# Rounding weights 512 columns at a time, and halving the first products of a fused attention and feed-forward kernel

## The chip, the cores and the metric

The kernel runs on one core of a Trainium2 chip. The metric is the device time of one execution in microseconds (us). The core has five engines that work side by side and wait for each other by semaphores: TensorE (PE in a profile, with its weight loads as PEld), VectorE (DVE), ScalarE (ACT), GpSimd (POOL), and SyncE (SP), which only issues DMAs here.

## What is computed

```python
# q, k, v: 8 batches x 8 heads x 576 rows x 64
scores = (q @ k.T) / 8
kth = the 32nd largest of each row of scores
attn = softmax(scores, with everything below kth masked out)
x = (attn @ v), rows of all batches below each other: 4608 x 512
g = x @ w_gate                      # 512 x 1536
out = ((g * sigmoid(g)) * (x @ w_val)) @ w_out      # w_out: 1536 x 512
```

q, k, v and the weights are random; the weights come as 64-bit floats, and the kernel rounds them to 32-bit ones on the chip.

## The kernel before

**Attention.** The work is cut into 160 units: (batch, query tile, pair of heads), with four tiles of 128 queries and a last one of 64 per batch, and four pairs of heads. A unit of the first four tiles has two heads (`nh` is 2); in a unit of the last tile, both heads lie in one set of 128 partitions, so it counts as one. The first batch's short units are 16 to 19. For a unit,

- `scores` (L276) makes the scores on TensorE (L306, or L292 for a short unit), and ScalarE copies them to `sc` (L311, L297);
- `select` (L314) finds the 32nd largest value on VectorE: four rounds of MAX8 (L327) with three of MATCH_REPLACE8 between them (L331), for each head, and then L337, which marks what lies below;
- `penalize` (L341) adds the marks to the scores on GpSimd (L349);
- `weigh` (L352) takes the exponentials on ScalarE (L358), and `normalize` (L366) divides by the sums (L370 on VectorE, L373 on ScalarE);
- `turn` (L375) transposes the result on TensorE (L385; ScalarE's copies are L386);
- `values` (L396) multiplies by v (L405, L414), and ScalarE copies the result into `xT[kb]` (L429). `done[kb]` counts the columns that are there.

`fetch` brings a batch's k and q: `load` issues the DMAs and `prep` transposes them on TensorE (L261, L253).

**Feed-forward.** The 4608 rows of x are 18 blocks of 256, which don't line up with the 576 rows of a batch. `feed(kb)` makes block kb: for each of six slices s of 256 hidden columns a gate product and a value product (`product`, L468, both [128 x 2 x 256] into a PSUM tile of `ps_f`, which has three), three ScalarE operations on the gate (L493 to L495), one on the value (L500), and two multiplications on GpSimd (L496, L501). Then comes the product with `wo`: plain for block 0 (L514), and in seven products of quarter size for the others (`quarter`, L554), with factors `T` that GpSimd makes from `wo` once. `feed` is a generator; each `yield` ends a piece and gives its size: 1 for four matmuls of 256 columns or two of 512, 0.75 for three of the quarters' matmuls.

**Rounding.** `rounded` (L105) takes one piece of a weight matrix, 128 rows x 256 columns, through five stages: the DMA (L109), two ScalarE operations (L114, L116), one on GpSimd (L119), one on VectorE and one on GpSimd (L123, L126), and a last one on VectorE (L129). `weights` makes 72 pieces, gate and value in turn for each 256 hidden columns and then `wo`, and sets them off as a pipeline: step n starts piece n and takes earlier ones through a later stage by `lags`. `ready[0]` counts the finished pieces. `rounding(n)` makes n steps; `need(n)` makes as many as it takes until n pieces are ready. `early[0]` moves the ScalarE stage of the newest pieces ahead. Loaded weights have six buffers `w`, and the sizes six.

**The order.** No scheduler moves anything: the four engines execute their instructions in the order in which the program names them. The loop at L705 makes one pass for each unit n; "step n" is that pass. In it stand, in this order: GpSimd's `penalize(n-1)`, TensorE's `turn(n-3)`, `values(n-4)` and `scores(n+1)`, ScalarE's `weigh(n-1)` and score copies, and then VectorE's `select(n)` in seven portions by `dve(k)`, between which pieces of the feed-forward work are placed by `pieces(k)`. `dve` lets 5/11 of a rounding step fall due for each selection operation, but none in the first four. `credit` limits the pieces: 4.45 are added in a step of two heads and 2.25 in a short one, and at most 8 are kept; from step 28 (`HEAD`) on `share(n)` takes the place of 4.45. ScalarE's and GpSimd's part of a product isn't placed at once but kept in `on_act` and `on_pool`, which `flush` empties; `piece` empties each of them first when it holds more than one entry:

```python
if len(on_act) > 1:
    flush(on_act)
if len(on_pool) > 1:
    flush(on_pool)
```

A block may begin when `done[kb]` says that all its columns are there. For block 0 these are units 0 to 7, which `values` finishes in step 11; for block 1 units 8 to 15 (step 19); block 2 takes in the last 64 rows of batch 0 and units up to 27 (step 31).

Of the kernel before, what the change touches and what calls it, by code (L numbers as in the profile page):

```python
# [8 lines left out]
AF = mybir.ActivationFunctionType  # L9
ALU = mybir.AluOpType  # L10
FP32 = mybir.dt.float32
I32 = mybir.dt.int32
# [3 lines left out]
P = 128  # L16
# [4 lines left out]
BLK = 256  # L21
WP = 256
# [5 lines left out]
def kernel(  # L28
# [37 lines left out]
    nc = tc.nc  # L66
    B, H, S, D = q.shape
    DM, DFF = w_gate.shape
# [17 lines left out]
    conv = ctx.enter_context(tc.tile_pool(name="conv", bufs=2))  # L86
# [17 lines left out]

    def rounded(src, dst):  # L105

        n = dst.shape[1]
        w = ffn.tile([P, n, 2], I32, tag="w", name="w", bufs=6)
        nc.sync.dma_start(w[:], src.bitcast(I32).rearrange("p (f t) -> p f t", t=2))  # L109
        yield  # L110
        low, high = w[:, :, 0], w[:, :, 1]

        size = conv.tile([P, n], FP32, tag="size", name="size", bufs=6)
# [9 lines left out]
        nc.vector.tensor_scalar(  # L123
            bits, bits, 3, 0x3FFFFFFF, ALU.logical_shift_left, ALU.bitwise_and
        )
        nc.gpsimd.tensor_tensor(bits, bits, low, ALU.add)  # L126
        yield

        nc.vector.scalar_tensor_tensor(  # L129
            out=dst.bitcast(I32), in0=high, scalar=-0x40000000, in1=bits,  # L130
            op0=ALU.bitwise_and, op1=ALU.bitwise_or,
        )

    def weights():

        pieces = []
        for f in range(0, DFF, WP):
            for src, dst in ((w_gate, wg), (w_val, wv)):
                for c in range(KC):
                    pieces.append((src[c * P : (c + 1) * P, f : f + WP], dst[:, c, f : f + WP]))  # L140
        for c in range(MC):
            for f in range(0, DM, WP):
                pieces.append((w_out[c * P : (c + 1) * P, f : f + WP], wo[:, c, f : f + WP]))
        pieces = [rounded(*p) for p in pieces]
        step = [0] * len(pieces)

        def upto(i, k):

            while 0 <= i < len(pieces) and step[i] < k:
                next(pieces[i], None)  # L150
                step[i] += 1

        lags = (5, 3, 2, 2, 0)
        for n in range(len(pieces) + lags[0]):
            for k, lag in enumerate(lags):
                upto(n - lag, len(lags) - k)
            ready[0] = max(n - lags[0] + 1, 0)
            early[0] = lambda: [upto(n - 1, 2), upto(n, 2)]
            yield
        early[0] = lambda: None  # L160


        add, sub = ALU.add, ALU.subtract
        lo, hi = slice(0, DM // 2), slice(DM // 2, DM)
        for m in range(0, MQ, 2):
            mm, nn = slice(m, m + 2), slice(MQ + m, MQ + m + 2)
            t3 = ffn.tile([P, 2, DM // 2], FP32, tag="w", name="t3", bufs=6)
            nc.gpsimd.tensor_tensor(t3[:], wo[:, nn, hi], wo[:, mm, hi], sub)
            T[7] += [t3[:, i, :] for i in range(2)]
            yield  # L170
        while not plain_done:
            yield
        for m in range(0, MQ, 2):
            mm, nn = slice(m, m + 2), slice(MQ + m, MQ + m + 2)
            t1 = wo[:, mm, hi]
            nc.gpsimd.tensor_tensor(t1, t1, wo[:, mm, lo], sub)
            T[5] += [wo[:, m + i, hi] for i in range(2)]
            yield
            t2 = ffn.tile([P, 2, DM // 2], FP32, tag="w", name="t2", bufs=6)
            nc.gpsimd.tensor_tensor(t2[:], wo[:, nn, hi], t1, sub)  # L180
            T[6] += [t2[:, i, :] for i in range(2)]
            yield
            for i in range(2):
                t4 = conv.tile([P, DM // 2], FP32, tag="size", name="t4", bufs=6)
                nc.gpsimd.tensor_tensor(t4[:], wo[:, MQ + m + i, lo], t2[:, i, :], sub)
                T[4].append(t4[:])
# [263 lines left out]
    def flush(queue):  # L450
        while queue:
            queue.pop(0)()

    def feed(kb):

        x = xT.pop(kb)
        hs = []  # L460

        def product(w, s, then):
            ps = ps_f.tile([P, 2, BLK], FP32, tag="f", name="f")
            need(8 * s + (4 if w is wg else 8))
            for i in range(2):
                m = 2 * s + i
                for kc in range(KC):
                    nc.tensor.matmul(  # L468
                        ps[:, i, :],
                        w[:, kc, m * P : (m + 1) * P],  # L470
                        x[:, kc, :],
                        start=(kc == 0),
                        stop=(kc == KC - 1),
                    )
                if i == 1:
                    on_act.append(lambda: then(ps))
                yield 1

        plain = kb == 0
        first, late = slice(0, P), slice(P, BLK)  # L480
# [2 lines left out]
            "p (m t) -> p m t", t=P  # L483
        )

        for s in range(MS):
            h = ffn.tile([P, 2, BLK], FP32, tag="h", name="h", bufs=MS + 1)
            hs.append(h)


            def gate(ps, h=h):
                half = ffn.tile([P, 2, BLK], FP32, tag="gv", name="half_g", bufs=3)
                nc.scalar.activation(h[:], ps[:], AF.Tanh, scale=0.5)  # L493
                nc.scalar.mul(half[:], ps[:], 0.5)
                nc.scalar.add(h[:], h[:], 1.0)  # L495
                on_pool.append(lambda: nc.gpsimd.tensor_mul(h[:], h[:], half[:]))  # L496

            def value(ps, h=h, s=s):
                val = ffn.tile([P, 2, BLK], FP32, tag="gv", name="val", bufs=3)
                nc.scalar.copy(val[:], ps[:])  # L500
                on_pool.append(lambda: nc.gpsimd.tensor_mul(h[:], h[:], val[:]))  # L501

            yield from product(wg, s, gate)
            yield from product(wv, s, value)
# [132 lines left out]
    current = []  # L637

    def piece():
# [4 lines that stand above are left out]
            flush(on_pool)  # L644
        while True:
            if not current:
                if not todo or done.get(todo[0], 0) < NHP * BLK:
                    return 0
                flush(on_act)
                flush(on_pool)  # L650
                current.append(feed(todo.pop(0)))
            cost = next(current[0], 0)
            if cost == 0:
                current.pop()
                continue
            return cost

    def fetch(n):

# [34 lines left out]
    load(1)  # L694
    run(fetch(0))
    run(scores(0))
    rounding(2)
    run(fetch(1))
    credit = [0.0]
    no = iter(())  # L700
    over = {}
    TURN, VALUES = 3, 4
    HEAD = 28
    due = [0.0]
    for n in range(NU + VALUES):  # L705
        nh = n_heads(units[n][1]) if n < NU else 1
        topk = select(n) if n < NU else no
# [106 lines left out]
```

## Time and profile before

| | us |
|---|---|
| device time, three runs | 1844.97, 1845.41, 1846.03 |
| the profiled run | 1845.35 |
| its span | 1843.6 |
| TensorE busy | 1708.1 (93%) |
| VectorE busy | 1623.5 (88%) |
| ScalarE busy | 1208.6 (66%) |
| GpSimd busy | 1026.2 (56%) |

Busy shares are means over stages with different limits. So the page also cuts the span into 40 slices of 46 us and gives the busy share of each engine in tenths (a digit 9 is 90% or more); PEclk in the same form is the clock that TensorE was granted. A table of windows gives, for each stretch, its length and then for PE, PEld, DVE, ACT and POOL the busy time with the number of instructions, then the granted clock, the busy share of the DMA engines and GB/s. The chain of work that ended last is followed back from the last instruction; its rows are start, length and what was done. A timeline has start, length, engine, line, operation, output and inputs, and in brackets how long the engine was idle before it, and what ended that. TensorE makes a matmul of 32-bit operands in two records, and a transpose in one.

### The profile page before, as it was taken

The page shows a single profiled execution, that of the slowest core. Times are in us where ns is not written, and L with a number is a line of the kernel's source. Part 1 is how long each engine was busy: PE and PEld are TensorE (multiplying, and loading weights), DVE is VectorE, ACT ScalarE, POOL GpSimd, SP SyncE. Part 2 cuts the span into 40 slices and gives each one's busy share as a digit, 9 for nine tenths or more (in the row PEclk, how much of TensorE's full clock was granted, in tenths as well). Part 3 has the DMA queues.
Part 4 walks back from the last instruction along what each step waited for, and adds up shares of the span by engine and source line. Part 5 has one row for each costly group of instructions (what it writes and reads, how often), then busy time and mean ns, then how long its engine had stood idle before and what let it go on. Part 6 is the DMA issues. An engine that isn't in the chain of part 4 may idle for free.

```text
span 1843.6 us, 30858 instructions
## 1 busy us (share of the span) xinstructions
PE 1708.1 (93%) x10756; PEld 1409.2 (76%) x10756; DVE 1623.5 (88%) x3477; ACT 1208.6 (66%) x3015; POOL 1026.2 (56%) x1007
## 2 busy tenths in 40 slices
PE   3447899999999989999999999999999999999998
PEld 2336658777788878887888878888788878888887
DVE  7999999999999979997999989998999989998400
ACT  5667757667666667676767675767676776675432
POOL 4666756645455644656464736564556554646444
PEclk7668999989999999999999999999999999999999
DMA  7332221000300021000300012000300011000000
GB/s 191 92 86 81 69 53 40 12 1 8 86 1 13 1 59 34 13 1 14 73 19 1 13 36 57 2 12 2 73 19 12 1 36 32 1 12 12 1 12 12
DMA packets 111260, 59.67 MB, mean 32 GB/s; under 512 B 89088, under 2 KB 97280, under 8 KB 111104
## 3 DMA queue, kind: packets, MB, share of 16 engines
q1 hardware_dynamic: 109904, 57.41, 11.8%
q8 instruction: 85, 1.39, 0.3%
q14 instruction: 71, 0.58, 0.1%
q10 hardware_dynamic: 1200, 0.30, 0.1%
HBM read 48.23 MB, written 9.44 MB: 31 GB/s over the span
## 4 chain that ended last, share of the span: by engine, by line
PE 83%; DVE 6%; ACT 3%; POOL 3%; issue 2%; DMA 0%; POOLq 0%; ACTq 0%
PE f L468 39%; PE x_ps L554 9%; PE av L414 8%; PE etps L385 7%; PE s L306 7%; PE y_ps L554 6%; DVE m L327 2%; DVE rest L331 2%; PE s L292 2%; PE av L405 1%; PE o_ps L514 1%; PE kqps L261 1%; POOL e L349 1%; ACT e L358 1%; DVE e L337 1%
## 5 line engine op out<-in xcount | busy, mean ns | idle before, releaser
L327 DVE MAX8 m<-rest 128x8 f32<-128x576 f32 x864 | 614.5, 745 | 2.2
L331 DVE MATCH_REPLACE8 rest<-m,rest 128x576 f32<-128x576 f32 x576 | 423.4, 741 | 0.0
L349 POOL TENSOR_TENSOR e<-e,sc 128x1152 f32<-128x1152 f32 (+1 forms) x160 | 382.7, 2392 | 67.2 <-DVE e L337 61.7
L468 PE MATMUL f<-xT,wg 128*128 128x256 f32 x1728 | 401.7, 382 | 0.0
L468 PE MATMUL f<-xT,wv 128*128 128x256 f32 x1728 | 398.9, 381 | 0.0
L468 PEld LDWEIGHTS f<-xT,wg 128*128 128x128 f32 x1728 | 322.8, 190 | 62.5 <-issue 20.5
L468 PEld LDWEIGHTS f<-xT,wv 128*128 128x128 f32 x1728 | 324.5, 190 | 58.5 <-issue 16.3
L496 POOL TENSOR_TENSOR h<-h,half_g 128x512 f32<-128x512 f32 x108 | 138.2, 1279 | 295.2 <-ACT h L495 289.6
L327 DVE MAX8 m<-sc 128x8 f32<-128x576 f32 x288 | 205.1, 748 | 99.1 <-ACT sc L297 58.3
L385 PE MATMUL etps<-ident,e 128*128 128x128 f32 (+1 forms) x1312 | 186.7, 287 | 104.3 <-POOL size L126 36.2
L358 ACT ACTIVATE e<-e,bias 128x576 f32<-128x576 f32 x288 | 222.1, 777 | 93.3 <-POOL e L349 93.2
L386 ACT COPY et<-etps 128x512 f32<-128x512 f32 (+1 forms) x448 | 184.3, 483 | 124.3 <-PE etps L385 122.9
L385 PEld LDWEIGHTS etps<-ident,e 128*128 128x128 f32 (+1 forms) x1312 | 159.6, 147 | 133.1 <-POOL size L126 39.0
L501 POOL TENSOR_TENSOR h<-h,val 128x512 f32<-128x512 f32 x108 | 140.2, 1298 | 193.2 <-ACT val L500 193.1
L373 ACT ACTIVATE e<-e,tot 128x576 f32<-128x576 f32 x288 | 211.9, 789 | 6.3 <-DVE tot L370 6.3
L331 DVE MATCH_REPLACE8 rest<-m,sc 128x576 f32<-128x576 f32 x288 | 211.6, 740 | 0.0
L306 PE MATMUL s<-kqT 64*128 64x288 f32 x1024 | 171.1, 447 | 4.4 <-ACT kqT L266 3.8
L414 PE MATMUL av<-et,v 128*64 128x128 f32 (+1 forms) x2560 | 173.8, 281 | 0.0
L337 DVE TENSOR_SCALAR e<-sc,m 128x576 f32<-128x576 f32 x288 | 165.4, 610 | 3.4
L311 ACT COPY sc<-s 128x288 f32<-128x288 f32 x512 | 163.9, 402 | 1.9 <-PE s L306 1.9
L414 PEld LDWEIGHTS av<-et,v 128*64 128x64 f32 x2560 | 136.8, 144 | 23.0 <-issue 7.1
L493 ACT ACTIVATE h<-f 128x512 f32<-128x512 f32 x108 | 65.4, 605 | 132.6 <-PE f L468 132.6
(71 smaller groups left out, 2042.1 us busy)
## 6 DMA issues: line engine op xcount, KB each, us to landing
kq_in<-in_k_dram SPq DMA_DIRECT2D x64, 128.0 KB, 2.8
v<-in_v_dram SPq DMA_DIRECT2D x32, 256.0 KB, 2.9
kq_in<-in_q_dram SPq DMA_DIRECT2D x62, 128.0 KB, 2.9
w<-in_moe_w_gate_dram SPq DMA_DIRECT2D x24, 256.0 KB, 2.7
w<-in_moe_w_val_dram SPq DMA_DIRECT2D x24, 256.0 KB, 2.7
w<-in_moe_w_out_dram SPq DMA_DIRECT2D x24, 256.0 KB, 2.5
out_dram<-o SPq DMA_DIRECT2D x40, 128.0 KB, 2.4
out_dram<-o SPq DMA_DIRECT2D x16, 256.0 KB, 2.4
```

The costliest lines, as they stand in the source:

```text
L306: nc.tensor.matmul(ps[:, 0:half], slab[d, q0 : q0 + P], slab[d, k0 : k0 + half])
L327: nc.vector.max(m[:, t, 8 * r : 8 * r + 8], cur[:, hs])
L331: nc.vector.match_replace(rest[:, hs], m[:, t, 8 * r : 8 * r + 8], cur[:, hs], LOWEST)
L337: nc.vector.tensor_scalar(e[:, hs], sc[:, hs], m[:, t, TOP_K - 1 : TOP_K], FAR, ALU.is_lt, ALU.mult)
L349: nc.gpsimd.tensor_tensor(e[:, every], e[:, every], sc[:, every], ALU.add)
L358: nc.scalar.activation(e[:, hs], e[:, hs], AF.Exp, bias=bias[:, t : t + 1], scale=scale, accum_out=tot[:, t : t + 1],)
L373: nc.scalar.mul(e[:, hs], e[:, hs], tot[:, t : t + 1])
L385: nc.tensor.transpose(ps[0:kl, c * P : (c + 1) * P], e[:, k0 : k0 + kl], ident[:])
L386: nc.scalar.copy(et[0:kl, c0 : c0 + cn, :], ps[0:kl, 0 : cn * P].rearrange("p (c j) -> p c j", c=cn),)
L414: nc.tensor.matmul(av[hh * R : (hh + 1) * R, 0:ql], v_last[:, hh, :] if c == J else vt[:, hh, c, :], moving, start=last and c == 0, stop=c ...
L468: nc.tensor.matmul(ps[:, i, :], w[:, kc, m * P : (m + 1) * P], x[:, kc, :], start=(kc == 0), stop=(kc == KC - 1),)
L554: nc.tensor.matmul(ps, lhsT, T[i][m], start=m == 0, stop=m == MQ - 1)
```

## The change

`rounded` takes pieces of twice the size: two row groups of 256 columns for gate and value weights, and a whole row group of 512 for `wo`. There are 36 of them, in three buffers of double size, and a step of the pipeline acts on a piece every second time, so that as many columns fall due as before. In the prelude k and q of the first pair of heads are split over the DMA queues by head, `rounding(2)` after the first scores is left out, and `due` starts at 2.0.

`parts` cuts the columns of blocks 0 and 1 into two halves of 128. `feed` makes all gate and value products of the first half and then those of the second, and a half may begin when its own columns are there: those of units 0 to 3 for block 0 (step 7), and of units 8 to 11 for block 1 (step 15). A half's piece has size 0.5, and `pieces` counts sizes, not pieces, so that two of 0.5 or two of 0.75 now go where one of 1 went.

`need`, which made rounding steps at once, becomes `until`, which yields 0 while weights are missing: then no piece is placed, and the next place for one tries again.

```diff
-        w = ffn.tile([P, n, 2], I32, tag="w", name="w", bufs=6)
+        w = ffn.tile([P, 2, WP, 2], I32, tag="w", name="w", bufs=3)
...
-                for c in range(KC):
-                    pieces.append((src[c * P : (c + 1) * P, f : f + WP], dst[:, c, f : f + WP]))
+                for c in range(0, KC, 2):
+                    rows = src[c * P : (c + 2) * P, f : f + WP]
+                    pieces.append((
+                        rows.rearrange("(c p) f -> p c f", p=P), dst[:, c : c + 2, f : f + WP]
+                    ))
...
-        for n in range(len(pieces) + lags[0]):
+        for n in range(2 * len(pieces) - 1 + lags[0]):
             for k, lag in enumerate(lags):
-                upto(n - lag, len(lags) - k)
-            ready[0] = max(n - lags[0] + 1, 0)
-            early[0] = lambda: [upto(n - 1, 2), upto(n, 2)]
+                if (n - lag) % 2 == 0:
+                    upto((n - lag) // 2, len(lags) - k)
+            ready[0] = max((n - lags[0]) // 2 + 1, 0)
+            early[0] = lambda: upto(n // 2, 2)
             yield
...
-    def need(n):
+    def until(n):
 
         while ready[0] < n:
-            next(weight)
+            yield 0
...
-            queue = nc.scalar if n == 1 and i == 0 else nc.sync
             for hh in range(2):
+                queue = nc.scalar if hh == 1 and i == 0 else nc.sync
                 queue.dma_start(
...
-            queue.dma_start(
+            nc.sync.dma_start(
                 kq_last[n * R : (n + 1) * R], src[b, h, JP:S].rearrange("h p d -> p h d")
...
+    def parts(kb):
+
+        return [slice(0, P), slice(P, BLK)] if kb < 2 else [slice(0, BLK)]
...
-        def product(w, s, then):
+        def product(w, s, c, then):
+            n = c.stop - c.start
+            yield from until(4 * s + (2 if w is wg else 4))
             ps = ps_f.tile([P, 2, BLK], FP32, tag="f", name="f")
-            need(8 * s + (4 if w is wg else 8))
...
-                yield 1
+                yield n / BLK
...
+        for c in parts(kb):
+            while done[kb] < NHP * c.stop:
+                yield 0
...
-                    need(8 * MS + 2 * m + 2)
+                    yield from until(4 * MS + m + 1)
...
-                if not todo or done.get(todo[0], 0) < NHP * BLK:
+                if not todo or done.get(todo[0], 0) < NHP * parts(todo[0])[0].stop:
                     return 0
...
     def pieces(n):
-        for _ in range(n):
-            if credit[0] >= 1:
-                credit[0] -= piece()
+        while n > 0 and credit[0] >= 1:
+            size = piece()
+            if not size:
+                break
+            n -= size
+            credit[0] -= size
...
-    rounding(2)
     run(fetch(1))
...
-    due = [0.0]
+    due = [2.0]
```

GpSimd's factors `T` get their room in the same three buffers (`room`), and its last subtraction, made for each of two row groups before, is made once for both.

More of the change, by code (lines that the diff above doesn't have):

```diff
@@ L105, in rounded @@
     def rounded(src, dst):
-        n = dst.shape[1]
-        w = ffn.tile([P, n, 2], I32, tag="w", name="w", bufs=6)
-        nc.sync.dma_start(w[:], src.bitcast(I32).rearrange("p (f t) -> p f t", t=2))
+        w = ffn.tile([P, 2, WP, 2], I32, tag="w", name="w", bufs=3)
+        nc.sync.dma_start(
+            w[:].rearrange("p c f t -> p c (f t)"), src.bitcast(I32)
+        )
         yield
-        low, high = w[:, :, 0], w[:, :, 1]
-        size = conv.tile([P, n], FP32, tag="size", name="size", bufs=6)
+        low, high = w[:, :, :, 0], w[:, :, :, 1]
+        size = conv.tile([P, 2, WP], FP32, tag="size", name="size", bufs=3)
         nc.scalar.activation(size[:], high.bitcast(FP32), AF.Abs)
@@ L138, in weights @@
             for src, dst in ((w_gate, wg), (w_val, wv)):
-                for c in range(KC):
-                    pieces.append((src[c * P : (c + 1) * P, f : f + WP], dst[:, c, f : f + WP]))
+                for c in range(0, KC, 2):
[3 more added lines that the diff above has]
+                    ))
         for c in range(MC):
-            for f in range(0, DM, WP):
-                pieces.append((w_out[c * P : (c + 1) * P, f : f + WP], wo[:, c, f : f + WP]))
+            pieces.append((
+                w_out[c * P : (c + 1) * P].rearrange("p (c f) -> p c f", c=2),
+                wo[:, c].rearrange("p (c f) -> p c f", c=2),
+            ))
         pieces = [rounded(*p) for p in pieces]
@@ L164, in weights @@
         lo, hi = slice(0, DM // 2), slice(DM // 2, DM)
+        room = []
+        for _ in range(3):
+            t = ffn.tile([P, 4, DM // 2], FP32, tag="w", name="t", bufs=3)
+            room += [t[:, 0:2], t[:, 2:4]]
         for m in range(0, MQ, 2):
             mm, nn = slice(m, m + 2), slice(MQ + m, MQ + m + 2)
-            t3 = ffn.tile([P, 2, DM // 2], FP32, tag="w", name="t3", bufs=6)
-            nc.gpsimd.tensor_tensor(t3[:], wo[:, nn, hi], wo[:, mm, hi], sub)
+            t3 = room.pop()
+            nc.gpsimd.tensor_tensor(t3, wo[:, nn, hi], wo[:, mm, hi], sub)
             T[7] += [t3[:, i, :] for i in range(2)]
@@ L178, in weights @@
             yield
-            t2 = ffn.tile([P, 2, DM // 2], FP32, tag="w", name="t2", bufs=6)
-            nc.gpsimd.tensor_tensor(t2[:], wo[:, nn, hi], t1, sub)
+            t2 = room.pop()
+            nc.gpsimd.tensor_tensor(t2, wo[:, nn, hi], t1, sub)
             T[6] += [t2[:, i, :] for i in range(2)]
             yield
[L183 to L186, printed above, removed]
+            t4 = conv.tile([P, 2, DM // 2], FP32, tag="size", name="t4", bufs=3)
+            nc.gpsimd.tensor_tensor(t4[:], wo[:, nn, lo], t2, sub)
+            T[4] += [t4[:, i, :] for i in range(2)]
             yield
@@ L222, in load @@
                 )
-            queue.dma_start(
+            nc.sync.dma_start(
                 kq_last[n * R : (n + 1) * R], src[b, h, JP:S].rearrange("h p d -> p h d")
@@ L452, in flush @@
             queue.pop(0)()
+    def parts(kb):
+        return [slice(0, P), slice(P, BLK)] if kb < 2 else [slice(0, BLK)]
     def feed(kb):
-        x = xT.pop(kb)
+        x = xT[kb]
         hs = []
-        def product(w, s, then):
+        def product(w, s, c, then):
+            n = c.stop - c.start
+            yield from until(4 * s + (2 if w is wg else 4))
             ps = ps_f.tile([P, 2, BLK], FP32, tag="f", name="f")
-            need(8 * s + (4 if w is wg else 8))
             for i in range(2):
@@ L468, in product @@
                     nc.tensor.matmul(
-                        ps[:, i, :],
+                        ps[:, i, 0:n],
                         w[:, kc, m * P : (m + 1) * P],
-                        x[:, kc, :],
+                        x[:, kc, c],
                         start=(kc == 0),
@@ L475, in product @@
                 if i == 1:
-                    on_act.append(lambda: then(ps))
-                yield 1
+                    on_act.append(lambda: then(ps[:, :, 0:n], c))
+                yield n / BLK
         plain = kb == 0
@@ L484, in feed, with gate, value @@
         )
[L486 to L504, printed above, removed]
+        for c in parts(kb):
+            while done[kb] < NHP * c.stop:
+                yield 0
+            for s in range(MS):
+                if c.start == 0:
+                    hs.append(ffn.tile([P, 2, BLK], FP32, tag="h", name="h", bufs=MS + 1))
+                h = hs[s]
+                def gate(ps, c, h=h):
+                    half = ffn.tile([P, 2, BLK], FP32, tag="gv", name="half_g", bufs=3)
+                    hc, gc = h[:, :, c], half[:, :, c]
+                    nc.scalar.activation(hc, ps, AF.Tanh, scale=0.5)
+                    nc.scalar.mul(gc, ps, 0.5)
+                    nc.scalar.add(hc, hc, 1.0)
+                    on_pool.append(lambda: nc.gpsimd.tensor_mul(hc, hc, gc))
+                def value(ps, c, h=h):
+                    val = ffn.tile([P, 2, BLK], FP32, tag="gv", name="val", bufs=3)
+                    hc, vc = h[:, :, c], val[:, :, c]
+                    nc.scalar.copy(vc, ps)
+                    on_pool.append(lambda: nc.gpsimd.tensor_mul(hc, hc, vc))
+                yield from product(wg, s, c, gate)
+                yield from product(wv, s, c, value)
+        del xT[kb]
         o = ffn.tile([P, 2, DM], FP32, tag="o", name="o", bufs=1)
@@ L651, in piece @@
                 current.append(feed(todo.pop(0)))
[L652 to L656, printed above, removed]
+            size = next(current[0], None)
+            if size is not None:
+                return size
+            current.pop()
     def fetch(n):
```

## The prediction

> **What bounds the kernel now.** I read part 2 of the page first, then windows of 20 us over the head, then groups, timeline and chain there. "Step n" is pass n of the loop at L705; it ends with VectorE's two L337 of unit n.
>
> ```profile
> PE   3447899999999989999999999999999999999998
> DVE  7999999999999979997999989998999989998400
> PEclk7668999989999999999999999999999999999999
> ```
>
> After its first tenth TensorE is full; before that it is not, while VectorE is.
>
> ```profile
> 100.00:120.00 20.00, 12.28 (x70) 9.85 (x70) 20.00 (x48) 14.42 (x39) 12.09 (x19) 0.60 0.36 104
> 120.00:140.00 20.00, 6.36 (x36) 5.13 (x37) 20.00 (x51) 12.63 (x34) 12.93 (x16) 0.65 0.29 79
> 140.00:160.00 20.00, 11.61 (x77) 9.66 (x78) 20.00 (x48) 14.49 (x40) 12.48 (x19) 0.75 0.33 108
> 160.00:180.00 20.00, 20.00 (x113) 17.22 (x112) 19.00 (x40) 13.29 (x33) 14.99 (x16) 1.00 0.17 54
> ```
>
> The third figure of busy time is VectorE: 20.00 of 20 up to 160 us. The feed-forward work starts at 158.8 us and fills TensorE. Reading VectorE's timeline step by step: step 31 starts at 380.9 us; steps 31 to 35 take 10.56 us each with no wait, a one-head step 6.25. With the 0.53 us that a rounded piece takes (below), the head's floor is 12.6 (VectorE's first start) + 27x10.56 + 4x6.25 + 72x0.53 = 361 us. So 20 us are lost up to 380.9: 4.0 in steps 0 to 10, 10.0 in 11 to 16, 5.2 in 17 to 30, and rounding.
>
> ```profile
> 354.23 0.98 PE etps L385 x9
> 355.21 0.22 PE av L405 x2
> 355.44 1.05 PE av L414 x16
> ...
> 365.27 1.17 PE s L306 x8
> 366.44 3.01 issue
> ...
> 383.47 1.71 PE f L468 x7
> ```
>
> In this chain no feed-forward row stands between 354 and 383 us: block 1 is done and block 2's columns need values of unit 27, made in step 31. So whatever block 1 gains is given back in a longer pause. The built order of the changed program bears this out: in steps 27 to 30 it has no product at all, from step 31 on TensorE has the same sequence as before but for four steps with an inner exchange. The change is worth what it does to the start of step 31, one for one.
>
> [...]
>
> ```profile
> 176.62 2.62 POOL L349 TENSOR_TENSOR e<-e,sc 128x1152 f32<-128x1152 f32 x1
> 177.35 2.17 DVE L129 SCALAR_TENSOR_TENSOR wo<-w,size 128x256 int32<-128x256 int32 x1
> 179.20 1.45 POOL L501 TENSOR_TENSOR h<-h,val 128x512 f32<-128x512 f32 x1
> 179.45 1.36 DVE L123 TENSOR_SCALAR size<-size 128x256 int32<-128x256 int32 x1
> ```
>
> The 0.40 us L129 takes 2.17 and ends with L349. [...] in the chain above TensorE's rows follow the program's order. [...] Trace: L129 starts 0.33 us before the next instruction, L123 0.20[...]. [...]
>
> **The change part by part.**
> (1) *512 columns a piece.* VectorE had 72 pairs at 0.33+0.20 us; it gets 36 at 0.60+0.33 (the same with twice the elements). 38.2-33.5 = 4.7 us saved, nearly all where VectorE is full. ScalarE and GpSimd save too (L114, L116 0.33 each to an estimated 0.55; L126 0.75 to 1.28 as L501's 512 columns take, L119 0.44 to 0.60), hidden behind VectorE. But GpSimd's add (L126), 1.28 us long then, starts as soon as L123 has ended, so where L337 comes right behind (units 3, 7 and 10), it waits some 1.2 us and not 0.7. Steps 0 to 6, which lose 2.7 now, lose an estimated 3.0.
> (2) *Prelude.* k and q split over SP's and ScalarE's queues: k's halves issue together (0.7 us each), 0.7 us earlier; kq_last's q half goes on SP behind the others, 0.6 us later. VectorE's first MAX8 no longer stands behind L123 (12.64 us), but its second wait, the first size operation, comes after fetch(1)'s copies on ScalarE: estimated 14.7 against 14.2 us with the same work done. Cost 0.5 (-0.7 to +1.5).
> (3) *DMAs.* Half as many, twice as large (512 KB), same bytes, three buffers for six. From a freed buffer to the size operation that needs its successor: issue and landing an estimated 4.6 (0.5, and 2.7 as the page's median plus 256 KB at its 191 GB/s), ScalarE 0.55, GpSimd 0.6, so 6 us against four rounding steps of 8 us. Nothing expected; up to 5 us lost. Queued behind it on SP are later loads and stores, 2.4 to 2.9 us to landing and due a step later.
> (4) *Halves.* Block 0 starts at step 7. A 256-column product record takes 0.216 us (8 in 1.73), a 128-column one 0.109 by the transposes: TensorE pays nothing. ScalarE's operation of 256 columns takes 0.33 us (L114's spacing) and of 512 0.49 (L493's), so a block's worth of 48 short for 24 long ones costs 4 us over ten steps; GpSimd's 0.75 twice for 1.28 costs 2.6. Both idle over 3 us a step. Upper bound, were loads to cost the 190 ns that their rows last: +31 us a block; the transposes exclude it nearly.
> (5) *A new order on GpSimd.* In step 8 (and 12, the same pattern for the second half) two half products fit into `pieces(2)`, so ScalarE's val and gate, and GpSimd's two multiplications, stand ahead of the size minimum of the next piece. In steps 7 and 11 eight such multiplications delay the 2.6 us add L349: as now in step 12, it starts 2.6 us into the step. From there in step 8: add ends 5.1, two exponentials 7.0, score copies 8.2, val and gate 9.5, multiplication 10.3, minimum 10.9 us. VectorE reaches the size operation that needs it after 8 selections and an L129: 6.2. It waits 4.7 us, twice: 9.4 (2.6 each if the add is on time, so 5 to 10). Other collisions and L337 in steps 7 to 16: 6.7 (the present 1.6 in 7 to 10 and 10.0 after it, with multiplications half as long).
> (6) *Not forced, due 2.0.* Forcing never happens in the steps that matter now: L129 runs 4 or 5 times in each. But w_out's twelve pieces now end at step 15: piece 10 after eight selections, piece 11 after thirteen (10.7 us into it). TensorE's order puts twelve o_ps matmuls into step 15, eleven of them not before that.
>
> ```profile
> 233.70 5.35 PE o_ps L514 x12
> 239.05 0.79 issue
> 239.84 1.38 PE etps L385 x9
> 241.22 0.22 PE av L405 x2
> 241.44 1.02 PE av L414 x16
> 242.47 1.12 PE s L292 x8
> ```
>
> Two records a matmul: 0.89 us. 11x0.89 = 9.8, so TensorE ends 20.5 us after step 15's start, 8.4 after step 16's. Then transposes 1.0, av 1.25, scores 1.1 and their copies 0.8: VectorE has its scores at 12.6, and wanted them at 6.25. It waits 6.3 us. TensorE then carries 6.1, 4.3, 4.5 and 4.5 us of products and transposes beside 3 of the unit's own in the short steps 16 to 19: further waits of 3.1, 1.3 and 1.4. Sum 12.1 (bounds 5, now, and 14). The two-head steps after it just keep pace (11 against 10.56 with the slack), and 27 to 30 have slack: 0.6.
> Sum up to step 31: floor 361-4.7+0.5 = 356.8; lost 3.0+9.4+6.7+12.1+0.6 = 31.8; 388.6 against 380.9: +7.7 us. The span of 1843.6 becomes 1851.3; its run was 1845.35, the others 1844.97 to 1846.03, so 1853.0 on their scale.
>
> **The rivals.**
> *Faster:* GpSimd's multiplications come in time and the o_ps burst is absorbed. VectorE keeps the 4.7, and TensorE, eleven pieces ahead by step 11, loses 1 us and not 5 in 17 to 30: 4.7-0.5+4 = 8 us, 1837. For it: VectorE is at 20.00 of 20, so each instruction saved there counts in full. Against: (5) and (6) follow from the order. It decides if VectorE's lost time up to step 31 stays below 20.0+4.7-0.5 = 24.2 us.
> *No change:* only one of (5) and (6) bites. Without (5), 7.7-9.4 = -1.7; without (6), 7.7-6.9 = +0.8: 1844 to 1846.
> *Slower yet:* both, and the larger DMAs arrive late in steps 1 to 6 (5 us), or half matmuls cost more than half: 1858 to 1863. TensorE's clock of 0.60 at 100 us speaks for it.
> *It doesn't do what it says* (no earlier start) is excluded: the 128-column rows stand ahead of step 8's transposes.
>
> **How the numbers follow.** Faster 0.20, no change 0.17, slower 0.63 (the forecast 0.48, slower yet 0.15). 0.2% (3.7 us) is about what a measurement can tell from no change. The range runs from 1840, inside the faster case, to 1862; about 2 in 10 lie outside.
>
> **What would show it.** Right: in the profile after, step 31 starts near 388 us with the rest as before; VectorE idles about 5 us before a size operation in steps 8 and 12 (releaser GpSimd's minimum), about 6 before a MAX8 in step 17 (releaser ScalarE's score copy); MAX8 stays at 0.745 us; 36 size operations at 0.33 to 0.45. Wrong: no such waits, or step 31 before 380; a difference made after step 31; 128-column product records spaced well over 0.11 us.

## The result, and the profile after

| | before | after |
|---|---|---|
| device time, median of five runs each, us | 1845.62 (1844.97 to 1846.03) | 1862.31 (1861.94 to 1864.73) |
| ratio, 95% interval | | 1.0092 (1.0078 to 1.0106) |
| span of the profiled run, us | 1843.6 | 1860.1 |
| start of step 31, us | 380.9 | 401.1 |

The changed kernel is slower by 16.7 us; 7.7 were forecast, and the range ended at 1862.0. Its direction was right and its size was not. Read off VectorE's timeline step by step (a step ends with its last marking, L349), the time went here (length of each stretch in us; the floor is VectorE's own work at 10.56 us a two-head step and 6.25 a one-head step):

| | before | after | difference |
|---|---|---|---|
| up to the end of step 6 | 105.9 | 103.0 | -2.9 |
| steps 7 to 16 | 134.8 | 139.1 | +4.3 |
| steps 17 to 20 (floor 29.3) | 31.1 | 46.2 | +15.1 |
| steps 21 to 30 (floor 105.6) | 109.1 | 112.8 | +3.7 |
| step 31 to the end | 1462.7 | 1459.0 | -3.7 |

In the table of windows of the changed kernel the third busy time is VectorE's again; before, it was 20.00 of 20 up to 160 us.

```profile
120.00:140.00 20.00, 11.64 (x79) 10.09 (x75) 14.69 (x32) 11.48 (x29) 14.05 (x14) 0.74 0.18 53
240.00:260.00 20.00, 20.00 (x138) 13.92 (x137) 8.32 (x15) 9.55 (x25) 5.69 (x6) 1.00 0.05 17
```

Two stretches now have VectorE idle: around 130 us with TensorE idle too, and around 250 us with TensorE at 20.00 of 20. The list of what VectorE waited for between 100 and 300 us (sum, times, longest) names two things:

```profile
DVE m L339 <- ACT sc L309: 13.7, 3, 8.8
DVE size L124 <- POOL size L120: 12.1, 5, 5.3
```

The second row is steps 8, 9 and 12, with 0.5 us in step 15. GpSimd's timeline of step 8, which begins at 118.4 us:

```profile
121.51 2.65 POOL L361 TENSOR_TENSOR e<-e,sc 128x1152 f32<-128x1152 f32 x1
124.11 1.20 POOL L518 TENSOR_TENSOR h<-h,half_g 128x256 f32<-128x256 f32 x1
127.77 0.73 POOL L524 TENSOR_TENSOR h<-h,val 128x256 f32<-128x256 f32 x1 [2.46 <-ACT val L523]
128.56 0.72 POOL L518 TENSOR_TENSOR h<-h,half_g 128x256 f32<-128x256 f32 x1
129.37 0.61 POOL L120 TENSOR_SCALAR size<-size 128x512 f32<-128x512 f32 x1
```

and VectorE's row that waits for the last of them, with the wait in brackets:

```profile
130.02 0.43 DVE L124 TENSOR_SCALAR size<-size 128x512 int32<-128x512 int32 x1 [5.31 <-POOL size L120]
```

The multiplications of step 7's products hold the add L361 until 121.51, 3.1 us into the step; the exponentials wait for the add, ScalarE's val (L523) stands behind the exponentials, and the minimum L120 behind that. The first row of the waits is steps 17 to 19. The chain after w_out's last pieces, where `233.70 5.35 PE o_ps L514 x12` was the longest run of o_ps before:

```profile
234.43 11.40 PE o_ps L538 x22
...
248.07 1.12 PE s L304 x8
```

Step 16 ended at 242.1, and VectorE got step 17's scores at 250.92. Of the chain ahead of block 2 this is left:

```profile
390.69 1.23 POOL e L361
...
403.00 8.83 PE f L485 x40
```

Block 2 begins right after step 31's start, as before, and from 358 to 403 us no product stands in the chain: blocks 0 and 1 are done early and nothing comes of it.

### The profile page after: what moved, and what is told of

It is laid out like the page before. It is cut to its first block, busy times and chain, and to the rows that moved or that the text cites. A ratio compares the mean times of both kernels' runs of the same rounds, so it can differ in the third digit from the quotient of the medians.

```text
span 1860.1 us, 31376 instructions
## 1 busy us (share of the span) xinstructions
PE 1719.8 (92%) x11140; PEld 1426.9 (77%) x11140; DVE 1616.4 (87%) x3405; ACT 1211.1 (65%) x2991; POOL 1020.6 (55%) x956
## 4 chain that ended last, share of the span: by engine, by line
PE 78%; POOL 3%; ACT 3%; DVE 2%; issue 1%; POOLq 0%; ACTq 0%; DVEq 0%
PE f L485 38%; PE x_ps L578 9%; PE av L426 7%; PE etps L397 7%; PE s L318 6%; PE y_ps L578 6%; PE s L304 2%; PE av L417 1%; DVE m L339 1%; DVE rest L343 1%; POOL e L361 1%; PE kqps L273 1%; PE o_ps L538 1%; ACT e L370 1%; POOL p L564 1%
## 5 line engine op out<-in xcount | busy, mean ns | idle before, releaser
L339 DVE MAX8 m<-rest 128x8 f32<-128x576 f32 x864 | 622.3, 765 | 2.2
L343 DVE MATCH_REPLACE8 rest<-m,rest 128x576 f32<-128x576 f32 x576 | 429.1, 761 | 0.0
L361 POOL TENSOR_TENSOR e<-e,sc 128x1152 f32<-128x1152 f32 (+1 forms) x160 | 382.9, 2393 | 82.6 <-DVE e L349 73.5
L485 PE MATMUL f<-xT,wv 128*128 128x256 f32 (+1 forms) x1920 | 408.1, 364 | 15.0 <-DVE wv L130 14.0
L485 PE MATMUL f<-xT,wg 128*128 128x256 f32 (+1 forms) x1920 | 406.9, 362 | 4.1 <-DVE wg L130 4.1
L485 PEld LDWEIGHTS f<-xT,wv 128*128 128x128 f32 x1920 | 337.0, 193 | 71.9 <-issue 18.3
L485 PEld LDWEIGHTS f<-xT,wg 128*128 128x128 f32 x1920 | 333.5, 191 | 62.2 <-issue 20.2
L518 POOL TENSOR_TENSOR h<-h,half_g 128x512 f32<-128x512 f32 (+1 forms) x120 | 141.7, 1181 | 308.0 <-ACT h L517 302.2
L524 POOL TENSOR_TENSOR h<-h,val 128x512 f32<-128x512 f32 (+1 forms) x120 | 143.5, 1196 | 199.5 <-ACT val L523 198.5
L385 ACT ACTIVATE e<-e,tot 128x576 f32<-128x576 f32 x288 | 212.3, 790 | 8.5 <-DVE tot L382 8.5
L349 DVE TENSOR_SCALAR e<-sc,m 128x576 f32<-128x576 f32 x288 | 170.7, 639 | 3.4
L515 ACT ACTIVATE h<-f 128x512 f32<-128x512 f32 (+1 forms) x120 | 67.9, 566 | 135.0 <-PE f L485 134.8
```

Source lines behind the costliest of these rows:

```text
L339: nc.vector.max(m[:, t, 8 * r : 8 * r + 8], cur[:, hs])
L343: nc.vector.match_replace(rest[:, hs], m[:, t, 8 * r : 8 * r + 8], cur[:, hs], LOWEST)
L349: nc.vector.tensor_scalar(e[:, hs], sc[:, hs], m[:, t, TOP_K - 1 : TOP_K], FAR, ALU.is_lt, ALU.mult)
L361: nc.gpsimd.tensor_tensor(e[:, every], e[:, every], sc[:, every], ALU.add)
L385: nc.scalar.mul(e[:, hs], e[:, hs], tot[:, t : t + 1])
L485: nc.tensor.matmul(ps[:, i, 0:n], w[:, kc, m * P : (m + 1) * P], x[:, kc, c], start=(kc == 0), stop=(kc == KC - 1),)
```

## The experiments

Theory A, the forecast's: the loss is one of order. Multiplications on GpSimd stand ahead of what VectorE needs (steps 8 and 12), o_ps comes as a burst (step 15), and GpSimd is late in steps 21 to 26; the larger pieces are a gain. Rivals: B, the larger pieces are slow themselves; C, half products cost an engine more than whole ones; D, the lost time would only move elsewhere. "Before" was measured beside each batch (1844.2 to 1844.7 us); on that scale the changed kernel is at 1861. All runs at a glance, lengths of the stretches in us from VectorE's timeline:

| run | median us | ratio to before, 95% | to step 6 | 7-16 | 17-20 | 21-30 | step 31 at |
|---|---|---|---|---|---|---|---|
| before | 1844.2 | | 105.9 | 134.8 | 31.1 | 109.1 | 380.9 |
| changed | 1861 (by the ratio) | 1.0092 (1.0078-1.0106) | 103.0 | 139.1 | 46.2 | 112.8 | 401.1 |
| x1_512_only | 1839.7 | 0.9974 (0.9966-0.9983) | 104.7 | 130.8 | 31.2 | 109.1 | 375.8 |
| x2_no_halves | 1836.7 | 0.9963 (0.9952-0.9975) | 104.4 | 130.8 | 31.3 | 109.0 | 375.5 |
| x3_256_halves | 1860.9 | 1.0094 (1.0077-1.0111) | 105.5 | 140.6 | 41.6 | 110.9 | 398.6 |
| x4_forced | 1859.2 | 1.0085 (1.0070-1.0100) | 104.1 | 148.1 | 34.9 | 110.4 | 397.5 |
| y1_minimum_first | 1860.0 | 1.0083 (1.0068-1.0099) | 104.0 | 135.4 | 47.0 | 112.9 | 399.3 |
| y2_o_ps_priced | 1851.0 | 1.0030 (1.0018-1.0043) | 104.3 | 140.0 | 32.2 | 112.6 | 389.1 |
| y3_both | 1850.2 | 1.0030 (1.0019-1.0041) | 104.1 | 136.3 | 31.9 | 112.6 | 384.9 |
| y4_block0_halved | 1860.8 | 1.0091 (1.0076-1.0106) | 104.7 | 140.5 | 39.9 | 115.0 | 400.1 |
| z1_burst_whole | 1845.4 | 1.0011 (1.0005-1.0018) | 104.1 | 130.8 | 40.0 | 108.9 | 383.8 |
| z2_no_factors | 1864.2 | 1.0110 (1.0095-1.0126) | 104.3 | 139.2 | 46.7 | 112.8 | 403.0 |
| z3_tamed | 1840.0 | 0.9977 (0.9968-0.9985) | 104.3 | 130.7 | 32.1 | 109.5 | 376.6 |
| z4_whole_minimum | 1837.2 | 0.9964 (0.9951-0.9977) | 104.1 | 130.3 | 31.2 | 109.1 | 374.7 |
| w1_count_only | 1855.6 | 1.0060 (1.0043-1.0076) | 104.3 | 130.8 | 45.7 | 110.5 | 391.3 |
| w2_count_and_price | 1840.6 | 0.9979 (0.9970-0.9987) | 104.1 | 130.3 | 31.4 | 109.5 | 375.3 |

**x1_512_only.** The kernel before with the changed kernel's `rounded` and `weights`:

```diff
-            need(8 * s + (4 if w is wg else 8))
+            need(4 * s + (2 if w is wg else 4))
-                    need(8 * MS + 2 * m + 2)
+                    need(4 * MS + m + 1)
```

> The kernel before with one part of the change alone: weights rounded 512 columns at a time (36 pieces, 3 buffers). Blocks stay whole, weights are still forced, the loads of the first units are as before. Theory A (the loss is one of order: GpSimd's queue in steps 8 and 12, the o_ps burst in step 15, GpSimd's ring in steps 21 to 26; the larger pieces by themselves are a gain): VectorE saves about 4.7 us, GpSimd's longer add gives some of it back, 1841 us (1838 to 1844). Rival B (the larger pieces themselves are slow: 512 KB loads late, GpSimd's 1.28 us add in everyone's way): 1848 to 1860 us. Rival C (half products cost TensorE, ScalarE or GpSimd more than whole ones): says nothing here, 1841 to 1846 us.

1839.7 us, step 31 5.1 us earlier: B is refuted. A row of VectorE's groups by line (count, busy time, mean ns, then idle time before):

```profile
L124 DVE TENSOR_SCALAR size<-size 128x512 int32<-128x512 int32 x36 | 15.0, 416 | 13.6 <-POOL size L120 13.6
```

36 operations of 416 ns stand for 72 of 296, and L130's 36 of 671 ns or more for 72 of 403 or more. All but 1.7 of the 13.6 us idle is the start of the span: with this prelude L124 is the first thing VectorE does after setting two tiles.

**x2_no_halves.**

```diff
-        return [slice(0, P), slice(P, BLK)] if kb < 2 else [slice(0, BLK)]
+        return [slice(0, BLK)]
```

> The changed kernel with the halves undone: every block's products are 256 columns wide, all else (512-column pieces, nothing forced, the first loads) stays. Theory A: no product stands in step 8, so its 5.3 us wait is gone; block 0 starts in step 11 and its o_ps no longer burst into step 15, GpSimd has no short multiplications in steps 20 to 26. 1840 to 1846 us, start of step 31 at 376 to 382 us. Rival B: stays at 1855 to 1862 us. Rival C: 1840 to 1846 us as A, but then a kernel with halves and no bad order must still be slow.

1836.7 us. All that makes the change slow, 25.6 us up to step 31, comes with the halves: +8.3 in steps 7 to 16, +14.9 in 17 to 20, +3.8 in 21 to 30, and -1.4 ahead of them. While the blocks are whole, `until` and the prelude cost nothing (x1 and x2 differ by 0.3 us at step 31); what `until` does to the halves is seen in x4.

**x3_256_halves.** The changed kernel with `rounded` and `weights` of the kernel before, and `until` with its numbers.

> The changed kernel with its weights rounded 256 columns at a time as before (72 pieces, 6 buffers); halves and nothing forced stay. Theory A: the same order trouble, plus 4 to 5 us of VectorE: 1864 to 1870 us, with waits for the size minimum in steps 8 and 12 and for scores in steps 17 to 19 still there. Rival B: the loss goes with the large pieces, 1845 to 1852 us. Rival C: about 1864 us, as A.

1860.9: the loss stays, against B. But A wanted 3 to 9 us more than in the changed kernel, and there is no difference to be seen: with halves, VectorE waits anyway, and what a shorter rounding saves goes into waits. They sit elsewhere (none in step 8, 3.2 us in step 12, 6.6 in step 18).

**x4_forced.**

```diff
         while ready[0] < n:
-            yield 0
+            next(weight)
```

> The changed kernel, but a product whose weights are missing forces their rounding again, as before the change. Theory A: w_out's rounding is no longer late, so the o_ps matmuls are spread over steps 12 to 16 and the score waits of steps 17 to 19 (14.6 us in the changed kernel) fall below 5; forced pieces instead make VectorE wait for loads in steps 8 and 12. 1850 to 1858 us, step 17's idle time of VectorE under 3 us. Rival C: the burst was not what cost, so 1860 us or more, with the time lost in other steps.

Half right: steps 17 to 20 fell to 34.9, and step 17 waited for nothing, as A says: without `until` there is no such burst. But forcing sets pieces off whose minimum comes late on GpSimd: VectorE waited 8.5 us for one in step 8, which took 32.5, and the gain was spent. 1859.2 is a microsecond above A's range.

**y1_minimum_first.**

```diff
-            early[0] = lambda: upto(n // 2, 2)
+            early[0] = lambda k=2: upto(n // 2, k)
...
             weigh(n - 1)
+            early[0](3)
```

> The changed kernel with the size minimum of the next piece issued on GpSimd right after the add and the exponentials of the step, ahead of the multiplications that the step's first products bring; nothing else moved. Theory A: the waits of 5.3, 1.7 and 4.6 us in steps 8, 9 and 12 shrink to about 1.3 in 8 and 12 (one multiplication still stands ahead), so step 13 ends 8 to 9 us earlier and the whole is 1852 to 1854 us on this scale (the kernel before 1844.2, the changed one 1861). Rival D (GpSimd and ScalarE are late whatever the order, the wait moves to the next instruction): 1858 us or more, the same idle time elsewhere in steps 8 to 16.

A miss, and inside D's range. Steps 7 to 16 gained 3.7 us, and the time hardly 1. GpSimd's timeline of step 8, which begins at 119.3 us here:

```profile
126.33 0.61 POOL L120 TENSOR_SCALAR size<-size 128x512 f32<-128x512 f32 x1
...
130.18 1.29 POOL L127 TENSOR_TENSOR size<-size,w 128x512 int32<-128x512 int32 x1
```

The minimum comes 7.0 us into the step and not 11.0, but the add L361 is as late as ever (at 122.46, 3.1 us into the step), so VectorE still waits 1.3 us for the minimum; and now the add L127 stands behind two multiplications, and VectorE waits 1.3 us for it too. So the place of the minimum is half of the wait in step 8, and the other half, as D says, moves on.

**y2_o_ps_priced.**

```diff
                     if m % 2 == 1:
-                        yield 1
+                        yield 2
```

> The changed kernel with block 0's o_ps matmuls priced at 2 credits a pair instead of 1 (they take some 1.9 us a pair, a product's four 128-column pairs 0.9): 4 of them instead of 12 come into step 15, and 2 into each later step. Theory A: VectorE's 15 us of score waits in steps 17 to 20 fall under 4; block 1 starts four steps later, but steps 27 to 30 have 17 us of idle TensorE to take it. 1849 to 1852 us. Rival D: the work left out there comes back as waits in steps 21 to 30, or delays block 1 past step 31: 1857 to 1862 us.

1851.0, in A's range: steps 17 to 20 fell by 14.0 us, and the waits in them to one of 2.4. Nothing came back in 21 to 30. The comparison of prices in the expectation misleads, though: four matmuls of 128 columns, 0.9 us, have size 0.5, so a pair of o_ps at 1.8 us and 1 credit was priced in proportion. The burst is credit that was kept, at most 8, while w_out was missing; at a price of 2 it lets four matmuls into step 15 (eight records in the trace) instead of twelve.

**y3_both.**

> The two edits together (minimum first, o_ps priced at 2). Theory A: the two losses are in different steps and add, so the gains add: 1840 to 1844 us, about as before the change; what is left above the kernel without halves (1836.7) is GpSimd's slowness in steps 21 to 26. Rival D: no better than the better of the two alone.

The gains add up to step 31 (384.9; 4.2 us before y2's), but the time is y2's: part was given back later, and A's range was missed by 6 us.

**y4_block0_halved.** `kb < 1` for `kb < 2` in `parts`.

> The changed kernel with the halves for block 0 alone; block 1's products are whole. Theory A: steps 8 and 12 and 17 to 19 wait as in the changed kernel; in steps 21 to 26 GpSimd has 12 multiplications of 1.3 us instead of 24 of 0.78, and ScalarE 48 operations less, and 2 to 5 of the 7 us lost there come back: 1856 to 1859 us. If the subtractions of the factors T alone make GpSimd late there: 1860 to 1862 us.

No gain. Block 1 starts later and its work presses on step 21 (a score wait of 3.8 us) instead of 18 to 20: from step 17 to 30, 154.9 us against 159.0, and 3.1 us are lost before that, spread over steps 0, 3, 12, 14 and 16. Taking the halves from block 1 alone gains nothing.

**z1_burst_whole.** The kernel without halves, with

```diff
                     yield from until(4 * MS + m + 1)
+                    while now[0] < 18:
+                        yield 0
```

where `now[0]` is the number of the step.

> The kernel without halves (512-column pieces, whole blocks) with block 0's o_ps matmuls held back until step 18, so that sixteen of them stand together there; otherwise the same. Theory A (a burst of o_ps in a one-head step makes VectorE wait for scores, halves or not): TensorE ends it some 16 us after step 18's start, the scores of unit 20 come some 20 us after it and are wanted at 12.5: a wait of 7 to 9 us in step 20 and smaller ones in 21 and 22, 1844 to 1850 us. Rival D (it is the short products and their 96 extra operations on ScalarE and GpSimd that make the score copies late): 1836 to 1840 us.

1845.4 us, 8.7 above x2. The chain of waits (sixteen matmuls of two records with one transpose of k and q between; the last twenty records and the scores are shown), and VectorE's only wait between 235 and 300 us:

```profile
251.50 8.59 PE o_ps L540 x20
...
261.88 1.17 PE s L318 x8
```

```profile
DVE m L339 <- ACT sc L323: 10.6, 1, 10.6
```

A burst of o_ps costs a score wait with no half product in the program: against D, and C is not needed for steps 17 to 20.

**z2_no_factors.** Each of the four subtractions is left out, and the list `T` takes the part of `wo` that it would have changed.

> The changed kernel without the twelve subtractions that make the factors T on GpSimd (the products take parts of w_out in their place, so the second to the last block are computed with other factors): 15 us less on GpSimd in steps 18 to 26. If these subtractions, ahead of the add and beside VectorE's marking, are what costs in steps 21 to 30: those take 107 to 109 us in place of 112.3, 1856 to 1858 us. If it is the short multiplications, or TensorE: 111 us and more, 1860 to 1862 us.

112.8 us in steps 21 to 30, to the tenth as with them: the factors are not what costs there. The time, 1864.2, is 2 us above the second range; 1.3 us of it are lost before step 7, where the program is the changed kernel's.

**z3_tamed.** y3, and in `pieces`

```diff
-            n -= size
+            n -= 1
```

which is how `pieces` counted before the change.

> Minimum first, o_ps priced at 2, and a half product counted as a whole one in the number of products that a place in the step takes: step 7 and step 11 get five half products for eight, so that fewer multiplications stand before the add of steps 8 and 12. Theory A: steps 7 to 9 and 11 to 12 lose 2 to 4 us less than with the two edits, 1846 to 1848 us; still above the 1837 us without halves, for nothing that block 0 and 1 gain is of use before unit 27's values. Rival D: no gain, 1850 us.

1840.0 us: far better than A's 1846 to 1848. Steps 7 to 16 fell by 5.6 us to what they take without halves, steps 21 to 30 by 3.1.

**z4_whole_minimum.** x2 with y1's edit.

> The kernel without halves, with the minimum first: VectorE's waits of 0.5, 0.1, 0.7 and 0.5 us for it in steps 9 and 11 to 13 should go, 1835 to 1837 us; a version to beat both kernels. If the add of the following piece collides with the marking instead, 1837 to 1839 us.

1837.2 us, between the two ranges and as x2: 0.8 us less at step 31, none that can be measured in the end. Both beat the kernel before by 7 us and the changed one by 24.

**w1_count_only and w2_count_and_price.** z3's edit alone on the changed kernel, and with y2's.

> The changed kernel with one edit: a half product counts as a whole one in the number of products that a place in the step takes (five half products in steps 7 and 11 for eight, none moved past its weights). If this order alone makes GpSimd's add late: steps 7 to 13 lose 7 to 8 us less, the o_ps burst in step 15 and its score waits stay, 1851 to 1855 us. If it works only together with the minimum's earlier place: 1858 to 1861 us.

> The half product counted as a whole one, and o_ps priced at 2; the minimum where the change put it. If the minimum's place does not matter once fewer multiplications stand before the add: 1839 to 1842 us, start of step 31 at 376 to 378 us, as with all three edits. If it does: 1844 to 1850 us, with a wait for the minimum of 2 us or more in steps 8 and 12.

w1: steps 7 to 16 at 130.8, all 8.3 us gone; the burst stays (45.7), and the time is 0.6 us above the range. w2 is as z3: with the old count, moving the minimum adds nothing. GpSimd in step 8 of w1, which begins at 119.1 us, and VectorE's row:

```profile
120.63 2.65 POOL L361 TENSOR_TENSOR e<-e,sc 128x1152 f32<-128x1152 f32 x1
123.23 0.74 POOL L524 TENSOR_TENSOR h<-h,val 128x256 f32<-128x256 f32 x1
123.92 0.74 POOL L518 TENSOR_TENSOR h<-h,half_g 128x256 f32<-128x256 f32 x1
124.75 0.98 POOL L120 TENSOR_SCALAR size<-size 128x512 f32<-128x512 f32 x1
...
127.58 0.73 POOL L524 TENSOR_TENSOR h<-h,val 128x256 f32<-128x256 f32 x1
```

```profile
125.76 0.43 DVE L124 TENSOR_SCALAR size<-size 128x512 int32<-128x512 int32 x1 [0.51 <-POOL size L120]
```

The wait is 0.5 and not 5.3, and the old count does two things for it. With five half products in step 7 for eight, the add starts 1.5 us into the step and not 3.1. And the place before the minimum takes one half product for two: the two multiplications between add and minimum are of step 7's products, whose inputs were ready, while the one whose val stands behind the exponentials on ScalarE, at 127.77 ahead of the minimum in the changed kernel, comes behind it here, at 127.58. No run brings the add in time and leaves the step's products ahead of the minimum, so the two are not weighed apart. The waits of w2 between 100 and 300 us, to be held against the two rows of the changed kernel:

```profile
DVE size L124 <- POOL size L120: 2.0, 4, 0.5
DVE m L339 <- ACT sc L309: 1.7, 1, 1.7
```

## Why the prediction was wrong in size, by its own steps

**(1) 512 columns: right.** 4.7 us forecast, 5.1 measured (x1 at step 31). The 0.60 and 0.33 us of the longer operations were the author's estimate; in the profile of after they take 0.59 and 0.34 from one start to the next (L130 at 201.40, L124 at 201.99, the next at 202.33). The collisions of steps 0 to 6 cost no more than forecast: the profile of after was 2.9 us ahead after step 6, the other kernels of that order 1.2 to 1.9, for step 3, at whose end GpSimd's add stands beside the markings, took 14.4 us in them (the markings 1.98 in y2) and, by luck, 13.4 in it (0.97). (The forecast's losses of before, 2.7 us in steps 0 to 6 and 1.6 in 7 to 10, do not add up to its 4.0 for 0 to 10; its own way of counting gives 3.0 and 1.4, so little hangs on it.)

**(2) Prelude: right within what can be seen.** A cost of 0.5 was forecast; at the end of step 0 x2, with the new prelude, is 0.3 us ahead of x1, and that point itself varies from 26.1 to 26.8 among kernels with one prelude. VectorE's first size operation, forecast at 14.7 us, began at 14.05.

**(3) DMAs: right.** The 512 KB pieces land in 3.6 to 3.8 us. ScalarE waited 18.2 us for them in all, in 13 waits, but none of these stands behind VectorE's waits in steps 8, 9 and 12.

**(4) Halves cost no engine time that matters: right.** 40 records of 128 columns take 4.46 us, 0.112 each (0.109 forecast, by transposes that have a load each: L385 has 1312 records of either kind in the profile before). Over both blocks ScalarE's operations on products take 39.8 us and not 29.7, GpSimd's multiplications 37.6 and not 31.0, so 5 and 3.3 us a block (4 and 2.6 forecast), and w2, which has them all, reaches step 31 as early as x2, which has none (375.3 and 375.5 us).

**(5) GpSimd's order: right in mechanism, and nearly in time.** 4.7 us each forecast for steps 8 and 12, 5.3 and 4.6 measured. The working named both things, the add that starts late behind step 7's eight multiplications and the two products ahead of the minimum. In step 8, taking the minimum past the products leaves half the wait (y1), undoing both a tenth of it (w1). What lies behind both is `pieces`, which counts sizes since the change and so lets twice as many half products into one place. The end of step 16, 242.1 us where the forecast's terms give 240.9, flatters the sum: steps 7 to 16 lost 18.6 us, not 16.1, most of the difference being the waits of 1.7 us in step 9, and steps 0 to 6 gave half of that back by the luck of step 3.

**(6) The burst: right mechanism, mis-sized.** Steps 17 to 20 lost 16.9 us (46.2 less 29.3) where 12.1 were forecast. Of the 8.8 us that the first score wait took (6.3 forecast), two parts that the sum did not have are seen. TensorE's burst was priced at 0.446 us a record, and 22 took 11.40, 0.518 each. Its windows show why (PE's busy time, then the granted clock):

```profile
234.00:236.00 2.00, 1.57 (x2) 0.66 0.00 0
236.00:238.00 2.00, 2.00 (x4) 0.50 0.07 26
```

TensorE had waited 3.9 us for w_out, and ran the first 3.4 us of the burst at half its clock (all of the second window, and by its mean of 0.66 some 1.4 us of the first). In the windows beside these it was at 1.00 (230 to 234 us, TensorE idle from 230.5 on) and 0.99 (238 to 240); what halved it and brought it back was not shown. And on ScalarE unit 15's exponentials, whose add had ended at 238.7, stood behind the copies of the late transposes, for which ScalarE was idle for 9.3 us, until 246.31, and ahead of the score copies.

```profile
249.05 0.77 ACT L370 ACTIVATE e<-e,bias 128x576 f32<-128x576 f32 x1
...
250.14 0.68 ACT L309 COPY sc<-s 128x288 f32<-128x288 f32 x2
```

The scores were there at 249.2, the copy began at 250.1: another microsecond. Steps 18 to 20 lost 7.7 us beyond their floor, not 5.8.

**The step that failed: "The two-head steps after it just keep pace (11 against 10.56 with the slack), and 27 to 30 have slack: 0.6".** Steps 27 to 30 did lose nothing, but 22 to 26 lost 7.2 us. Only TensorE's load had been reckoned, and 3.5 us that were lost in steps 21 to 30 before the change (3.4 in x2) were taken as gone without a reason. It is not the same loss, though. Before, the wait of step 26 came from TensorE: ScalarE's exponentials stood behind the copies of TensorE's late transposes, when GpSimd's add had ended at 322.0.

```profile
321.89 1.24 ACT L386 COPY et<-etps 128x512 f32<-128x512 f32 x3 [1.58 <-PE etps L385]
...
323.86 0.78 ACT L358 ACTIVATE e<-e,bias 128x576 f32<-128x576 f32 x1
...
326.80 1.42 DVE L327 MAX8 m<-sc 128x8 f32<-128x576 f32 x2 [1.58 <-ACT sc L311]
```

After, it came from GpSimd: its sums stood ahead of the add, the exponentials waited for that, and the score copies stood behind them.

```profile
340.35 2.10 POOL L626 TENSOR_TENSOR h<-h,xT 128x256 f32<-128x256 f32 x3
...
342.59 2.64 POOL L361 TENSOR_TENSOR e<-e,sc 128x1152 f32<-128x1152 f32 x1
```

```profile
345.26 0.78 ACT L370 ACTIVATE e<-e,bias 128x576 f32<-128x576 f32 x1 [3.21 <-POOL e L361]
```

```profile
348.21 1.42 DVE L339 MAX8 m<-sc 128x8 f32<-128x576 f32 x2 [2.24 <-ACT sc L323]
```

With the old count (w1), steps 22 to 24, where the last half products of block 1 are worked off, lose 2.2 us less, and 25 and 26, where its quarters stand, 4.4 as in the changed kernel. With o_ps priced at 2 as well (w2), 3.9 us are left in 21 to 30, hardly more than before. So what the change added there goes with the two orders; the way from w1 to w2 was not traced to one instruction.

Together: 1.2 us to step 16, 4.8 in 17 to 20 and 6.6 in 21 to 30 make up, but for rounding, the 12.5 us by which step 31 (401.1) came after the forecast's 388.6. **"The rest as before"** held within 3.7 us: from step 31 to the end all these kernels take 1458 to 1464 us. What sets which is open; a large part is in steps 141 to 145, which take from 53.1 to 57.2 us, in x2 and z4, the same program there, 57.2 and 53.1 (x2's profile is of its slowest run, 1840.2, and z4's of its fastest, 1834.8). It is why gains of 1 to 4 us at step 31 (y1, y3, z4) are not all found again in the medians. One cause stands untested: kernels whose `pieces` counts pieces (before, x1, z3, w1, w2) take 1461 to 1463 us, and those that count sizes 1458 to 1461 but for x2 and y3, and this count acts on the pieces of 0.75 in all later blocks too. It could be why the median of w2 is 3.9 us above that of x2, with step 31 at the same time. One of the signs named also failed without meaning: MAX8's mean record was 0.765 us, not 0.745, while a two-head step with no wait took 10.56 us as before.

**The faster rival** failed at its own point: VectorE's losses up to step 31 would have had to stay below 24.2 us, and were 44.3. It names what was possible all the same: with both orders mended (w2), or with whole blocks (x2), the loss falls to 18.5 or 18.7 us and the kernel is faster by 4 to 7 us. "No change" failed because both (5) and (6) bit. "Slower yet" gave the right size by the wrong cause: beside those two it wanted late loads or dear half matmuls, and there were none.

## What to carry to other kernels

When work is cut finer, look at everything that counts pieces: places that took two pieces now take four, with twice the operations on ScalarE and GpSimd. And look at what is kept while data is missing: credits saved until the weights came let eleven matmuls, 11.4 us of TensorE, out at once, just ahead of the short steps. Where an engine takes its operations in the program's order, as ScalarE did here (idle until 246.31 with exponentials behind whose add had ended at 238.7), ask what the new operations stand ahead of, on every engine up to the one that bounds the kernel, and look at the longest operation behind them too (here a 2.6 us add), not only at the one that is seen to be waited for: moving that one alone (y1) gave 3.7 us of 8.3, taking operations from before both (w1) all of them. A loss that the profile already shows in a stretch is kept in the sum until something is named that takes it away, and work that is brought forward is worth nothing if the next block waits for data that comes no sooner.

## What the hardware showed

- TensorE's clock was granted at 0.50 for some 3.4 us after a stall of 3.9 us, and a burst of 22 records took 11.40 us; 20 records of the same kind without a stall ahead took 8.59 (z1), 0.43 each. So the stall was paid again here, just when TensorE's work was late: with 1.9 us, by an estimate from these figures (11.40 less 22 of 0.43).
- The multiplication of 128x256 on GpSimd took 0.73 us, but 1.20 beside VectorE's L130 (0.86 us, alone 0.67). In the kernel before, VectorE's L129 took 2.17 us beside GpSimd's add of 2.62, and ended 0.28 us after it; alone it took 0.40. Why the operations are longer side by side, no trace here shows.
- VectorE's two markings at the end of step 3 took 0.97 us in the profile of the changed kernel, and GpSimd's add of a rounded piece, started 0.25 us after the first of them, took 1.86. In y2, with the same instructions up to there and 0.21 us between, the markings took 1.98 and the add 1.45. So one program order gave two results, 1.0 us apart on the engine that bounds the kernel; what decides between them was not shown.
